# Windowed attention and a gated feed-forward on one core: values placed behind the next group's scores, sink values in two row halves, group 4 one unit sooner

## The chip, the core and the metric

The kernel runs on one core of a Trainium2 chip. The core has five engines with an instruction queue each: TensorE (PE) multiplies matrices, VectorE (DVE) and ScalarE (ACT) work on elements, GpSimd (POOL) and SyncE (SP) here mainly issue DMAs. Matmuls write to PSUM, which has eight banks of 128 partitions x 512 fp32 numbers. DMAs of all issuers run on 16 DMA engines; a DMA can also transpose a bf16 tile on its way, by the crossbar (xbar). The metric is the device time of one execution in microseconds (us); less is better. All times below are us unless marked ns.

## The reference

Inputs: q, k, v of 4 batches x 8 heads x 768 tokens x 64, and the weights of a gated feed-forward, 512 to 1536 and back. `n_sink` is 4, `window` is 128.

```python
keep = is_sink | in_window          # the first 4 keys, or the last 128 up to the query
scores = np.where(keep, scale * q @ k.T, -1e9)
a = softmax(scores)
x = (a @ v) as (4*768, 8*64)        # heads side by side
g = x @ w_gate
out = (g * sigmoid(g) * (x @ w_val)) @ w_out
```

## The kernel before

Attention goes in 12 groups of 256 query tokens; group g is third g%3 (called c) of batch g//3. The feed-forward goes in eight blocks `tb` of 256, 256, 256, 512, 512, 512, 512 and 256 tokens (`SIZES`): block 3 takes groups 3 and 4, block 4 takes 5 and 6, and so on. All orders are written by hand (`manual_schedule`): each engine runs its instructions in the order in which Python emits them.

A group's steps:

- Transposes of q and k: on TensorE (`step_T`) for groups 0 to 3, by a crossbar DMA issued by SyncE (`cross_T`, L301, tiles `kqT`) from group 4 on.
- `step_S(g, p2)`, scores of four heads (L331). Two heads run at once, each on 64 rows of the array. They take four PSUM banks `s`; ScalarE's exps (L338) empty these into `e`; VectorE's mask multiplications (L343) follow.
- `step_K(g)`, scores of the four sink keys of all heads (L358), with an exp into `es` (L362). Groups with c = 0 have none, since their sinks are in the window's tiles or in the mask.
- `step_PV(g, j, hh)`, values for half j of the group's tokens (128) and half hh of its heads (4), in one bank `o` (L384): where c > 0 a 128-row matmul of `es` with the sink values `vsb` (128x260), then eight matmuls of `e` with `va` (128x65; four where there is no earlier key tile). VectorE takes the reciprocal of the row sums (L389) and writes the scaled rows to `xn` (L396). `xn` has three buffers, one for each (g, j).
- The transpose of `xn` into the feed-forward's input `xT`: on TensorE (`step_X`, L420, bank `px`, and a copy) for groups below `NXPE` = 5 other than 3; by a crossbar DMA from SyncE (L402) for 3 and from 5 on.

A *gate unit* `gate(tb, f)` of a 512-token block is pg (four matmuls, L448), tanh `th` on ScalarE (L455), then pv (four matmuls, L448), and on VectorE `u` (L462, from `th` and pg) and `ht` (L463, from `u` and pv). A *down unit* `down(tb, ts)` is 12 matmuls over `ht` (L501), a scaled copy on ScalarE and a store. A block of 512 has units 0 to 11 (gates) and 12 to 15 (downs).

`weave` runs the units and puts attention steps into them: into a gate unit between pg and pv, into a down unit among its matmuls. `slots` says which steps go into which unit. A step's VectorE work is put on the list `later`, and is emitted (`flush`) after the unit's `u` and `ht`. So VectorE's order in a unit with scores and values is u, ht, masks, rcp, xn. In block 3 a values step of one (j, hh) stands in each of the units 6 to 9, in order (0,0), (1,0), (0,1), (1,1); scores of the group after stand in 8 and 10. PSUM tiles of all kinds share eight buffers (`bank`); a new tile takes one whose last reader has been emitted, longest ago first, and its first matmul waits for that reader.

The first group has its own code ahead of the blocks: transposes, scores, values, with `warm(n)`, n matmuls of zeros 512 wide whose result nobody reads, at places where TensorE waits. The list `us` then mixes blocks 0 to 2 (gates of 256 tokens, two chunks each) by hand; its units 15 to 20 are block 2's gates, 21 and 22 block 1's downs, 23 and 24 block 2's. There groups 1 to 4 have their steps: scores of group 4 in units 20 and 21, its values in 22 and 23, its transposes in 24.

Of the kernel before, what the change touches and what calls it, by code (L numbers as in the profile page):

```python
# [8 lines left out]
FP32 = mybir.dt.float32  # L9
# [6 lines left out]
def kernel(  # L16
# [12 lines left out]
    nc = tc.nc  # L29
    P = 128  # L30
    B, H, S, D = q.shape
# [9 lines left out]
    GC = S // 256  # L41
# [2 lines left out]
    assert sum(SIZES) == NTOK and NG == 12 and S == 768  # L44
    OFF = [sum(SIZES[:i]) for i in range(len(SIZES))]
    NPE = 4
    NXPE = 5
    VS = 72
    FCH = [2, 2, 2, 2, 4]
    assert sum(FCH) == DFC  # L50
# [29 lines left out]
    def bank(shape, dtype, name):  # L80
        return psum.tile(shape, dtype, tag="b", name=name)
# [70 lines left out]
    vsbs, kss = [], []  # L152
# [77 lines left out]
    kTs, qTs, es_t, e_t, xns, xTs = {}, {}, {}, {}, {}, {}  # L230
    later = []

    def A(fn, *a):
        return lambda: fn(*a)
# [6 lines left out]
    def warm(n):  # L241

        ps = bank([P, 512], FP32, "wm")
        for _ in range(n):
            nc.tensor.matmul(ps, wm[:, 0:P], wm, start=True, stop=True)
# [36 lines left out]
    def keys(b, t, r, p):  # L282

        g, j = b * GC + t // 2, t % 2
        if g < NPE:
            return kTs[g][r, p, j * P:(j + 1) * P]
        return cross[g][r, j, 0, p]

    def queries(g, r, p, j, n):

        if g < NPE:
            return qTs[g][r, p, j * P:(j + n) * P]
        return cross[g][r, j:j + n, 1, p]
# [3 lines left out]
    def cross_T(g):  # L297

        t = crossp.tile([P, 2, 2, NP2, P], BF16, tag="kqT", name="kqT")
        for j in range(2):  # L300
            nc.sync.dma_start(  # L301
                t[:, j].rearrange("q i a m -> q (i a) m"),
                nat[g][:, j].rearrange("p i x -> p (i x)"), transpose=True)
        cross[g] = t
# [10 lines left out]
    def step_S(g, p2, mid=None):  # L315

        b, c = divmod(g, GC)
        if p2 == 0:
            e_t[g] = epool.tile([P, H, 512], BF16, tag="e", name="e")

        parts = [(2 * c, 0, 2, P), (2 * c + 1, 1, 1, 3 * P)]
        if c > 0:
            parts.insert(0, (2 * c - 1, 0, 1, 0))
        lo = 0 if c > 0 else P
        pss = [bank([P, 512], FP32, "s") for _ in range(4)]
        for pp in range(2):
            p = 2 * p2 + pp
            for t, j, n, col in parts:
                for h in range(2):
                    r = slice(h * D, (h + 1) * D)  # L330
                    nc.tensor.matmul(  # L331
                        pss[2 * pp + h][:, col:col + n * P], keys(b, t, r, p),
                        queries(g, r, p, j, n), start=True, stop=True)
        m = (mask if c > 0 else mask0).rearrange("q (o a) x -> q o (a x)", o=1)
        for pp in range(2):
            h0 = 4 * p2 + 2 * pp
            for h in range(2):
                nc.scalar.activation(  # L338
                    e_t[g][:, h0 + h, lo:512], pss[2 * pp + h][:, lo:512],
                    AF.Exp, scale=scale)  # L340

            def dve(e=e_t[g][:, h0:h0 + 2, lo:512]):
                nc.vector.tensor_tensor(  # L343
                    e, e, m[:, :, lo:512].broadcast_to([P, 2, 512 - lo]), op=ALU.mult)
            later.append(dve)
            if pp == 0 and mid:
                mid()
# [17 lines left out]

    def step_PV(g, j, hh, act=False):
        b, c = divmod(g, GC)
        t = 2 * c + j
        if hh == 0:
            xns[g, j] = xnp.tile([P, DM], BF16, tag="xn", name="xn")  # L370
        po = bank([P, 4, D + 1], FP32, "o")
        mms = []
        if c > 0:
            mms.append((po, es_t[g][:, j * P:(j + 1) * P],
                        vsbs[b][:, 4 * hh:4 * hh + 4]))
        for hq in range(4):
            h = 4 * hh + hq
            if t > 0:
                vp = vas[g][:, 0, h, 0:D + 1] if j else vas[g - 1][:, 1, h, 0:D + 1]
                mms.append((po[:, hq], e_t[g][:, h, 256 * j:256 * j + P], vp))  # L380
            mms.append((po[:, hq], e_t[g][:, h, 256 * j + P:256 * (j + 1)],
                        vas[g][:, j, h, 0:D + 1]))
        for i, (o, l, r) in enumerate(mms):
            nc.tensor.matmul(o, l, r, start=(i == 0), stop=(i == len(mms) - 1),  # L384
                             skip_group_check=True)

        def dve():
            rcp = smallp.tile([P, 4, 1], FP32, tag="rcp", name="rcp")
            nc.vector.reciprocal(rcp, po[:, :, D:D + 1])  # L389
            if act:  # L390
                for h in range(4):
                    nc.scalar.activation(  # L392
                        xns[g, j][:, (4 * hh + h) * D:(4 * hh + h + 1) * D],
                        po[:, h, 0:D], AF.Copy, scale=rcp[:, h])
                return
            nc.vector.tensor_tensor(  # L396
                xns[g, j][:, 256 * hh:256 * (hh + 1)].rearrange(
                    "p (h d) -> p h d", h=4),
                po[:, :, 0:D], rcp.broadcast_to([P, 4, D]), op=ALU.mult)
        later.append(dve)  # L400
        if hh == 1 and (g >= NXPE or g == 3):
            later.append(lambda: nc.sync.dma_start(  # L402
                x_tile(g, j), xns[g, j], transpose=True))

# [3 lines left out]
    def x_tile(g, j):  # L408

        t0 = g * 256 + j * P  # L410
        tb = max(i for i in range(len(SIZES)) if OFF[i] <= t0)
        if t0 == OFF[tb]:
            xTs[tb] = xtp.tile([P, 4, DMC, P], BF16, tag="xT", name="xT")
        return xTs[tb][:, (t0 - OFF[tb]) // P]
# [99 lines left out]
    def gates(tb):  # L514
        return [(gate, tb, f) for f in range(0, DFC, 512 // SIZES[tb])]

    def downs(tb):
        return [(down, tb, t) for t in range(SIZES[tb] // P)]
# [6 lines left out]
    def sinks(b):  # L525
        return [lambda: later.append(A(step_ks, b))]
# [7 lines left out]
    def Ss(g):  # L534
        return [A(step_S, g, p2) for p2 in range(2)]

    def PVs(g):

        return [A(step_PV, g, j, hh) for hh in range(2) for j in range(2)]

    def Xs(g):
        return [A(step_X, g, j) for j in range(2)]

    def K(g):
        return A(step_K, g)
# [5 lines left out]
    def weave(us, slots):  # L551
        assert all(i < len(us) for i in slots)
        for i, (fn, tb, x) in enumerate(us):
            fn(tb, x, slots.get(i, []))
# [7 lines left out]
    def slots(*pairs):  # L562
        sl = {}
        for at, steps in pairs:
            for i, step in zip(at if isinstance(at, tuple) else (at,) * len(steps),
                               steps):
                sl.setdefault(i, []).append(step)
        return sl

    def C(g):  # L570

        def last():
            cross_T(g)
            next_load(g)
        return [last]
# [4 lines left out]
    def first_T(ph):  # L580
        transpose(0, ph, lambda i, p: first[p] if i else nat[0][:, 2 * p:2 * p + 2],
                  (ident, id32))

    build_masks()
    first_T(0)
    step_S(0, 0, A(first_T, 1))
    warm(1)
    step_S(0, 1)
    warm(2)
    last_mask = later.pop()  # L590
    flush()

    step_PV(0, 0, 0, True)
    step_PV(0, 1, 0, True)
    later.insert(1, last_mask)


# [3 lines left out]
    for i in range(3, 5):  # L601
        load_gate(i)
    step_PV(0, 0, 1)
    step_PV(0, 1, 1)
    step_T(1, 0, q_act=True)
    flush()
# [18 lines left out]
    def first_PVs():  # L625
# [8 lines left out]
    us = [g0[0], (held_gate, 0, 2), (alone, 0, 0), g0[2], *g1[0:3], g0[3], *g1[3:6], *g0[4:6],  # L634
          *downs(0), *g2, *downs(1), *downs(2)]
    weave(us, slots(
        (0, [flush, A(step_S, 1, 1), K(1), A(next_load, 1)]), (2, [first_PVs]),
        (3, [A(step_X, 1, 0), A(step_X, 1, 1, True), flush]),
        (9, T(2)), ((10, 11), Ss(2)), (10, [K(2)]),
        (12, PVs(2)[:2] + [flush]), (13, PVs(2)[2:] + [flush]), (13, C(4)),  # L640
        (14, [A(step_X, 2, 0), A(step_X, 2, 1, True), flush]),
        (15, T(3)), ((16, 17), Ss(3)), (17, sinks(1)), ((18, 18, 19, 19), PVs(3)), (19, [flush]),
        (18, C(5)), ((20, 21), Ss(4)), (21, [K(4)]),
        ((22, 22, 23, 23), PVs(4)), (24, Xs(4))))

    def pair(ga, gb, sh=0):
        s = sh
        return [((s, s + 2), Ss(ga)), ((s + 4, s + 5, s + 6, s + 7), PVs(ga)),
                ((s + 6, s + 8), Ss(gb)),
                ((11, 11, 12, 12) if s else (10, 11, 12, 13), PVs(gb))]  # L650

    weave(gates(3) + downs(3), slots(
        (2, [K(5)]), *pair(5, 6, 2), (2, C(6)), (7, C(7)), (13, C(8))))
    weave(gates(4) + downs(4), slots(
        (0, sinks(2)), *pair(7, 8), (3, [K(7)]), (3, C(9)), (7, C(10)), (10, C(11))))
    weave(gates(5) + downs(5), slots(
        (0, sinks(3)), *pair(9, 10), (6, [K(10)])))
    weave(gates(6) + gates(7) + downs(6) + downs(7), slots(
        ((0, 2), Ss(11)), ((4, 5, 6, 7), PVs(11))))


# [33 lines left out]
```

The softmax here doesn't subtract the row's maximum and nothing guards it: scores larger than these inputs give would overflow.

## Time and profile before

The time is 242.3 us (median of three runs, 241.95 to 242.7); the profiled execution has a span of 240.4.

| engine | busy | share of the span | instructions |
|---|---|---|---|
| TensorE matmul | 232.7 | 97% | 2071 |
| TensorE weight load (beside the matmuls) | 135.3 | 56% | 2071 |
| VectorE | 158.8 | 66% | 334 |
| ScalarE | 112.6 | 47% | 227 |
| GpSimd | 70.7 | 29% | 92 |

The costliest groups on TensorE are pg and pv (74.2 and 74.4 busy) and pd (63.4); the o matmuls have 18.2 for values and 8.8 for sinks, the px transposes 3.5. The granted TensorE clock is 0.71 from 12 to 13 us, 0.50 from 13 to 15, 0.58 from 15 to 16 and full otherwise. Busy times of matmuls overlap, since the next starts before the one ahead has drained: start-to-start times tell what a matmul costs. In lines of the timeline the columns are start, time to the last end, engine, line, operation with out<-in, and, in brackets, the engine's idle time before it and what ended that.

### The profile page before, as it was taken

How to read it: one execution, taken by the hardware profiler on the slowest of the kernel's cores; microseconds unless marked ns; L12 is line 12 of the kernel's file. 1: busy time of each engine (PE TensorE's matmuls, PEld its weight loads, DVE VectorE, ACT ScalarE, POOL GpSimd, SP SyncE). 2: the span in 40 equal slices, each digit the busy share in tenths (PEclk: the TensorE clock that was granted, in tenths of full speed). 3: DMA queues.
4: the chain of work that ended last, by engine and by line, in shares of the span. 5: the costliest groups of instructions: out<-in, count | busy, mean ns of one | idle time of the engine just before them, and what ended most of it. 6: DMA issues, size and time to landing. Idle time of an engine off the chain costs nothing.

```text
span 240.4 us, 5190 instructions
## 1 busy us (share of the span) xinstructions
PE 232.7 (97%) x2071; PEld 135.3 (56%) x2071; DVE 158.8 (66%) x334; ACT 112.6 (47%) x227; POOL 70.7 (29%) x92
## 2 busy tenths in 40 slices
PE   7799999999999999999999999999999999999994
PEld 3477887768745445454445454445454445488443
DVE  4569778939973589880698971498971599877000
ACT  2778447358451483621656611556611662332111
POOL 8985387686256745650000000000000000000000
PEclk9979999999999999999999999999999999999999
DMA  7999999999999999999920654200304200200132
GB/s 136 147 180 197 206 187 206 171 154 145 194 119 200 195 160 155 155 148 191 236 48 0 125 97 133 87 0 1 46 0 131 90 0 3 44 0 3 59 117 87
DMA packets 98793, 27.37 MB, mean 114 GB/s; under 512 B 84817, under 2 KB 95825, under 8 KB 98769
## 3 DMA queue, kind: packets, MB, share of 16 engines
q0 software_dynamic: 68832, 13.90, 71.5%
q1 hardware_dynamic: 29504, 12.75, 26.9%
q10 hardware_dynamic: 432, 0.39, 0.5%
q8 instruction: 16, 0.26, 0.5%
q14 instruction: 9, 0.07, 0.1%
HBM read 28.34 MB, written 6.29 MB: 144 GB/s over the span
## 4 chain that ended last, share of the span: by engine, by line
PE 87%; DVE 5%; ACT 3%; DMA 2%; issue 1%; DVEq 0%; ACTq 0%; POOLq 0%
PE pv L448 25%; PE pd L501 25%; PE pg L448 23%; PE o L384 5%; PE s L331 4%; PE pt L267 3%; ACT e L338 2%; DVE e L343 2%; DMA kq<-in_k_dram 2%; DVE ht L463 1%; DVE xn L396 1%; PE px L420 1%; DMA out_dram<-ot 1%; DVE u L462 1%; ACT xn L392 1%
## 5 line engine op out<-in xcount | busy, mean ns | idle before, releaser
L448 PE MATMUL pv<-xT,wv 128*128 128x256 bf16 (+1 forms) x384 | 74.4, 326 | 0.2 <-DVE xn L396 0.2
L448 PE MATMUL pg<-xT,wg 128*128 128x256 bf16 (+1 forms) x384 | 74.2, 326 | 0.0
L455 ACT ACTIVATE th<-pg 128x512 f32<-128x512 f32 x72 | 43.9, 609 | 59.7 <-PE pg L448 59.3
L462 DVE SCALAR_TENSOR_TENSOR u<-th,pg 128x512 bf16<-128x512 f32 x72 | 49.2, 683 | 30.5 <-ACT th L455 29.7
L501 PE MATMUL pd<-wo,ht 128*128 128x512 bf16 x276 | 63.4, 379 | 0.0
L463 DVE TENSOR_TENSOR ht<-u,pv 128x512 bf16<-128x512 bf16 x72 | 49.5, 687 | 10.2 <-PE pv L448 3.3
L448 PEld LDWEIGHTS <-wg 128*128 128x128 bf16 x384 | 37.4, 98 | 25.4 <-issue 0.2
L338 ACT ACTIVATE e<-s 128x512 bf16<-128x512 f32 (+1 forms) x96 | 46.3, 583 | 1.2 <-PE s L331 1.1
L448 PEld LDWEIGHTS <-wv 128*128 128x128 bf16 x384 | 34.1, 98 | 20.6 <-issue 2.7
L501 PEld LDWEIGHTS <-ht 128*128 128x128 bf16 x276 | 25.8, 98 | 28.0 <-issue 0.2
L505 ACT ACTIVATE ot<-pd 128x512 f32<-128x512 f32 x23 | 13.7, 597 | 53.0 <-PE pd L501 52.9
L343 DVE TENSOR_TENSOR e<-e,mask 128x1024 bf16<-128x1024 bf16 (+1 forms) x48 | 28.9, 641 | 1.2 <-ACT e L338 1.0
L123 POOL DMA_DIRECT2D va<-in_v_dram x24 | 21.2, 885 | 12.6 <-DMA kq<-in_q_dram 5.7
L384 PEld LDWEIGHTS <-e 128*128 128x128 bf16 x352 | 16.6, 99 | 6.7 <-DVE vcf L598 0.7
L396 DVE TENSOR_TENSOR xn<-o,rcp 128x256 bf16<-128x256 f32 x44 | 18.7, 424 | 2.5 <-DMA xT<-xn 1.0
L384 PE MATMUL o<-va,e 128*128 128x65 bf16 x352 | 18.2, 195 | 0.9 <-DVE vcf L598 0.5
L107 POOL DMA_DIRECT2D kq<-in_k_dram x16 | 14.1, 883 | 8.6 <-DMA kqT<-kq 4.5
L107 POOL DMA_DIRECT2D kq<-in_q_dram x16 | 14.1, 883 | 6.1 <-DMA va<-in_v_dram 2.9
L389 DVE RECIPROCAL rcp<-o 128x4 f32<-128x4 f32 x48 | 8.4, 176 | 6.8 <-PE o L384 6.8
L486 DVE TENSOR_SCALAR ot<-pd 128x256 f32<-128x256 f32 x1 | 0.4, 425 | 14.4 <-DMA out_dram<-ot 14.4
L331 PE MATMUL s<-kqT 64*128 64x128 bf16 (+1 forms) x168 | 9.4, 238 | 0.0
L272 DVE CAST qT<-pt 128x512 bf16<-128x512 f32 x7 | 4.7, 689 | 6.9 <-PE pt L267 6.9
(61 smaller groups left out, 107.5 us busy)
## 6 DMA issues: line engine op xcount, KB each, us to landing
out_dram<-ot SPq DMA_DIRECT2D x23, 256.0 KB
va<-in_v_dram POOLq DMA_DIRECT2D x24, 128.0 KB, 10.3
kq<-in_k_dram POOLq DMA_DIRECT2D x18, 128.0 KB, 9.3
kq<-in_q_dram POOLq DMA_DIRECT2D x16, 128.0 KB, 9.4
wo<-in_moe_w_out_dram POOLq DMA_DIRECT2D x4, 384.0 KB, 12.7
wg<-in_moe_w_gate_dram POOLq DMA_DIRECT2D x4, 256.0 KB, 8.7
wv<-in_moe_w_val_dram POOLq DMA_DIRECT2D x4, 256.0 KB, 9.1
kq<-in_k_dram POOLq DMA_DIRECT2D x3, 256.0 KB, 9.6
```

Of the source, the lines that this page charges most:

```text
L107: nc.gpsimd.dma_start(x[:, j, i].rearrange("p (h d) -> p h d", d=D), src[b, :, t0:t0 + P].rearrange("h m d -> m h d"))
L123: nc.gpsimd.dma_start(va[:, j, :, 0:D], v[b, :, t0:t0 + P].rearrange("h m d -> m h d"))
L331: nc.tensor.matmul(pss[2 * pp + h][:, col:col + n * P], keys(b, t, r, p), queries(g, r, p, j, n), start=True, stop=True)
L338: nc.scalar.activation(e_t[g][:, h0 + h, lo:512], pss[2 * pp + h][:, lo:512], AF.Exp, scale=scale)
L343: nc.vector.tensor_tensor(e, e, m[:, :, lo:512].broadcast_to([P, 2, 512 - lo]), op=ALU.mult)
L384: nc.tensor.matmul(o, l, r, start=(i == 0), stop=(i == len(mms) - 1), skip_group_check=True)
L396: nc.vector.tensor_tensor(xns[g, j][:, 256 * hh:256 * (hh + 1)].rearrange("p (h d) -> p h d", h=4), po[:, :, 0:D], rcp.broadcast_to([P, 4, ...
L448: nc.tensor.matmul(ps[:, i * n:(i + 1) * n], ws[fi][:, c, fo * P:(fo + 1) * P], x[:, 0:n // P, c], start=(c == 0), stop=(c == DMC - 1))
L455: nc.scalar.activation(th, pg, AF.Tanh, scale=0.5)
L462: nc.vector.scalar_tensor_tensor(u, th, 1.0, pg, op0=ALU.add, op1=ALU.mult)
L463: nc.vector.tensor_tensor(hts[tb][:, f:f + two].rearrange("p a n -> p (a n)"), u, pv, op=ALU.mult)
L501: nc.tensor.matmul(po, hts[tb][:, f, ts * P:(ts + 1) * P], wos[f // n][:, f % n], start=(f == 0), stop=(f == DFC - 1))
```

## The change

Five edits, all in the order or form of attention work:

1. A new `step_PV2(g, j)` takes both head halves of a token half. Where c > 0 it first issues the two sink matmuls with 64 rows each (heads 0 to 3 lie on rows 0 to 63 of `es` and `vsb`, heads 4 to 7 on rows 64 to 127), so that they can run side by side as the scores do, then the values of both halves.
2. From block 3 on, `step_PV2` replaces the four `step_PV`, and where it can it stands behind the scores of the following group in the same unit, so that the array, still split by rows, takes the sinks as well. The last scores and values move from block 6 into block 5.
3. Group 4's scores, sink scores and values come one unit sooner, and its output goes by crossbar DMA (`NXPE` = 3) and no more by `step_X`.
4. Fillers: `warm(3)` after the first transposes, `warm(3)` for `warm(1)`, `warm(2)` and `warm(3)` among group 0's values.
5. In unit 0 of `us`, K(1) stands ahead of scores (1,1).

```diff
-    NXPE = 5
+    NXPE = 3
...
+    def step_PV2(g, j):
+        b, c = divmod(g, GC)
+        pos = [value_bank(g, j, hh) for hh in range(2)]
+        if c > 0:
+            for hh in range(2):
+                r = slice(64 * hh, 64 * (hh + 1))
+                nc.tensor.matmul(
+                    pos[hh], es_t[g][r, j * P:(j + 1) * P],
+                    vsbs[b][r, 4 * hh:4 * hh + 4],
+                    start=True, stop=False, skip_group_check=True)
+        for hh in range(2):
+            values(g, j, hh, pos[hh])
...
-        if hh == 1 and (g >= NXPE or g == 3):
+        if hh == 1 and g >= NXPE:
...
     first_T(0)
+    warm(3)
     step_S(0, 0, A(first_T, 1))
-    warm(1)
+    warm(3)
     step_S(0, 1)
     warm(2)
...
     step_PV(0, 0, 0, True)
     step_PV(0, 1, 0, True)
+    warm(2)
...
     step_PV(0, 0, 1)
+    warm(3)
     step_PV(0, 1, 1)
...
-        (0, [flush, A(step_S, 1, 1), K(1), A(next_load, 1)]), (2, [first_PVs]),
+        (0, [flush, K(1), A(step_S, 1, 1), A(next_load, 1)]), (2, [first_PVs]),
...
-        (18, C(5)), ((20, 21), Ss(4)), (21, [K(4)]),
-        ((22, 22, 23, 23), PVs(4)), (24, Xs(4))))
-
-    def pair(ga, gb, sh=0):
-        s = sh
-        return [((s, s + 2), Ss(ga)), ((s + 4, s + 5, s + 6, s + 7), PVs(ga)),
-                ((s + 6, s + 8), Ss(gb)),
-                ((11, 11, 12, 12) if s else (10, 11, 12, 13), PVs(gb))]
+        (18, C(5)), ((19, 20), Ss(4)), (20, [K(4)]),
+        ((21, 21, 22, 22), PVs(4))))
+
+    def PV2s(g):
+        return [A(step_PV2, g, j) for j in range(2)]
 
     weave(gates(3) + downs(3), slots(
-        (2, [K(5)]), *pair(5, 6, 2), (2, C(6)), (7, C(7)), (13, C(8))))
+        (2, [K(5)]), ((2, 4), Ss(5)), (2, C(6)), (7, C(7)),
+        ((8, 10), Ss(6)), ((8, 10), PV2s(5)), ((11, 12), PV2s(6)), (13, C(8))))
     weave(gates(4) + downs(4), slots(
-        (0, sinks(2)), *pair(7, 8), (3, [K(7)]), (3, C(9)), (7, C(10)), (10, C(11))))
+        (0, sinks(2)), ((0, 2), Ss(7)), (3, [K(7)]), (3, C(9)),
+        ((6, 8), Ss(8)), ((6, 8), PV2s(7)), (7, C(10)), (10, C(11)),
+        ((10, 12), Ss(9)), ((10, 12), PV2s(8))))
     weave(gates(5) + downs(5), slots(
-        (0, sinks(3)), *pair(9, 10), (6, [K(10)])))
-    weave(gates(6) + gates(7) + downs(6) + downs(7), slots(
-        ((0, 2), Ss(11)), ((4, 5, 6, 7), PVs(11))))
+        (0, sinks(3)), ((1, 3), PV2s(9)), ((2, 4), Ss(10)), (5, [K(10)]),
+        ((7, 9), Ss(11)), ((7, 9), PV2s(10)), ((11, 12), PV2s(11))))
+    weave(gates(6) + gates(7) + downs(6) + downs(7), {})
```

More of the change, by code (lines that the diff above doesn't have):

```diff
@@ L367, in step_PV, with value_bank, values @@
         b, c = divmod(g, GC)
-        t = 2 * c + j
+        po = value_bank(g, j, hh)
+        if c > 0:
+            nc.tensor.matmul(
+                po, es_t[g][:, j * P:(j + 1) * P], vsbs[b][:, 4 * hh:4 * hh + 4],
+                start=True, stop=False, skip_group_check=True)
+        values(g, j, hh, po, act)
+    def step_PV2(g, j):
+        b, c = divmod(g, GC)
+        pos = [value_bank(g, j, hh) for hh in range(2)]
+        if c > 0:
+            for hh in range(2):
+                r = slice(64 * hh, 64 * (hh + 1))
+                nc.tensor.matmul(
+                    pos[hh], es_t[g][r, j * P:(j + 1) * P],
+                    vsbs[b][r, 4 * hh:4 * hh + 4],
+                    start=True, stop=False, skip_group_check=True)
+        for hh in range(2):
+            values(g, j, hh, pos[hh])
+    def value_bank(g, j, hh):
         if hh == 0:
             xns[g, j] = xnp.tile([P, DM], BF16, tag="xn", name="xn")
-        po = bank([P, 4, D + 1], FP32, "o")
+        return bank([P, 4, D + 1], FP32, "o")
+    def values(g, j, hh, po, act=False):
+        b, c = divmod(g, GC)
+        t = 2 * c + j
         mms = []
-        if c > 0:
-            mms.append((po, es_t[g][:, j * P:(j + 1) * P],
-                        vsbs[b][:, 4 * hh:4 * hh + 4]))
         for hq in range(4):
@@ L383, in step_PV @@
         for i, (o, l, r) in enumerate(mms):
-            nc.tensor.matmul(o, l, r, start=(i == 0), stop=(i == len(mms) - 1),
-                             skip_group_check=True)
+            nc.tensor.matmul(o, l, r, start=(c == 0 and i == 0),
+                             stop=(i == len(mms) - 1), skip_group_check=True)
         def dve():
```

## The prediction

> **What bounds the kernel now.** I read the page first, then the waits of TensorE, then TensorE, VectorE and ScalarE in order of time in the three blocks of 512 tokens (78.7 to 211 us).
>
> ```profile
> PE 232.7 (97%) x2071; PEld 135.3 (56%) x2071; DVE 158.8 (66%) x334; ACT 112.6 (47%) x227; POOL 70.7 (29%) x92
> ...
> PE 87%; DVE 5%; ACT 3%; DMA 2%; issue 1%; DVEq 0%; ACTq 0%; POOLq 0%
> ```
>
> TensorE is busy for 97% of the span and is 87% of the chain that ended last. Its own waits (all named ones together 4.2 us) lie before 25 us, but for 0.2 us at 64.6. So after 25 us the end moves by what is taken from TensorE's work, or put into it as waits. TensorE in block 4:
>
> ```profile
> 118.61 1.03 PE L448 MATMUL pg<-xT,wg 128*128 128x512 bf16 x4
> 119.57 0.62 PE L331 MATMUL s<-kqT 64*128 64x128 bf16 x12
> 120.12 1.04 PE L448 MATMUL pv<-xT,wv 128*128 128x512 bf16 x4
> 120.99 1.03 PE L448 MATMUL pg<-xT,wg 128*128 128x512 bf16 x4
> ...
> 123.16 1.03 PE L448 MATMUL pg<-xT,wg 128*128 128x512 bf16 x4
> 124.02 0.27 PE L384 MATMUL o<-vsb,es 128*128 128x260 bf16 x1
> 124.13 0.41 PE L384 MATMUL o<-va,e 128*128 128x65 bf16 x8
> 124.38 1.02 PE L448 MATMUL pv<-xT,wv 128*128 128x512 bf16 x4
> ```
>
> Read starts only. Half a gate (4 matmuls) is 0.865 (120.12 to 120.99). So pg of 118.61 is through at 119.475; scores come 0.095 later (119.57), run 0.43 (1024 columns at the dense rate) and give back after another 0.12 (120.12): 0.65 in all. A values step is 0.36: sinks 0.11 and eight times 0.031. Beside it, VectorE and ScalarE:
>
> ```profile
> 97.54 0.69 DVE L463 TENSOR_TENSOR ht<-u,pv 128x512 bf16<-128x512 bf16 x1 [0.45 <-PE pv L448]
> 98.14 0.17 DVE L389 RECIPROCAL rcp<-o 128x4 f32<-128x4 f32 x1
> 98.35 0.42 DVE L396 TENSOR_TENSOR xn<-o,rcp 128x256 bf16<-128x256 f32 x1
> 98.69 1.02 DVE L343 TENSOR_TENSOR e<-e,mask 128x768 bf16<-128x768 bf16 x2
> 99.63 0.68 DVE L462 SCALAR_TENSOR_TENSOR u<-th,pg 128x512 bf16<-128x512 f32 x1
> 100.41 0.69 DVE L463 TENSOR_TENSOR ht<-u,pv 128x512 bf16<-128x512 bf16 x1
> ```
>
> ```profile
> 95.78 0.60 ACT L455 ACTIVATE th<-pg 128x512 f32<-128x512 f32 x1 [1.48 <-PE pg L448]
> 96.40 1.64 ACT L338 ACTIVATE e<-s 128x384 bf16<-128x384 f32 x4
> ```
>
> VectorE keeps program order. u to ht is 0.79, ht to the next 0.60 (1.39 a gate), a mask 0.47 (0.60 at 1024 wide), rcp and xn 0.55, xn written 0.62 after rcp starts. ht starts 0.20 after its pv ends (97.34), and masks and xn stand behind it. th starts 0.20 after pg ends (95.58), the exps behind it.
>
> ```profile
> 72.88 0.42 DVE L396 TENSOR_TENSOR xn<-o,rcp 128x256 bf16<-128x256 f32 x1 [1.04 <-DMA xT<-xn]
> ```
>
> ```profile
> 64.02 2.51 SPq L402 DMA_TRANSPOSE xT<-xn  x2
> ```
>
> These two say how slow the crossbar is here: xn has 3 buffers, so this xn (group 4, second half of tokens) waits for group 3's first transpose, issued at 64.02 and landed at 72.8: 8.8 us.
>
> **What the Trainium skill says.** "TensorEngine Tiling (Array Packing)", Key Properties: changing the tiling mode drains TensorE. The trace agrees: 0.10 into and about 0.12 out of 64-row scores. "TensorE: Matmul & The Clock Gate", Part 1: the clock halves when the array was little used over a window of about 3.4 us. The trace agrees: clock 0.50 to 0.71 between 12 and 16 us, after the gaps of 9 to 12. "DMA: Bandwidth & Descriptors", Issuing engines are not separate DMA queues: transfers of all issuers interleave on the same 16 engines. The trace agrees: 8.8 us above, with GpSimd's loads running, against 2.5 us for the one issued at 136.63 after they ended.
>
> **The change part by part.**
>
> *Row-shared sinks.* Two sink matmuls of 0.11 become two of 64 rows at once: 0.11 saved per step. Seven of the ten with sinks stand behind scores and share their drains: -0.77. Three ((8,1), (11,0), (11,1)) stand alone and pay 0.20 for entering and leaving: +0.09 each. Together **-0.5**.
>
> *Values behind scores.* The matmuls are the same, but one unit now takes pg, four score banks, two value banks and pv: all eight PSUM banks. VectorE gets 1.39+1.20+1.10 = 3.69 us in it, TensorE has 2.97. The built program shows whose release each matmul waits for:
>
> - Block 4 units 8 and 10, block 5 unit 9: the second sink matmul takes the bank of this unit's first score tile, so it waits for the first exp. That ends 0.20+0.60+0.03+0.60 = 1.43 after pg ends (1.33 for 384 columns); TensorE is there after 0.095+0.43 = 0.53 (0.42). With 0.05 for the release that is 0.92 to 0.96 each: **+2.8**. Behind it are 16 values matmuls, then pv.
> - Block 3 unit 10: the second sink matmul takes unit 9's pg bank, freed by u. With pg of unit 8 at 0: pv8 ends 2.87, ht8 3.07, masks 3.67, rcp/xn 4.61, u9 5.71, written 6.39. TensorE is there at 5.88: **+0.55**.
> - Block 3 unit 11: values of group 6, heads 4 to 7, need the masks of unit 10. From pv10's end: ht 0.20, masks at 0.80 and 1.27, written 1.78. TensorE, after pg and 4 matmuls, is there at 0.99: **+0.8**. Before, heads 0 to 3 of both token halves came in this slot and heads 4 to 7 a unit later.
> - Block 5 unit 4: pv waits for ht of unit 3, which xn of unit 1 and masks of unit 2 delay: **+0.2**.
>
> *Group 4 a unit sooner.* Two transposes by TensorE go (76.48 to 76.71 and 77.57 to 77.80): -0.46, the wait at 64.6 with the score half before it (-0.37), one mode change around K (-0.1). New: scores of group 4 stand behind group 3's last values, and the pv behind them takes the bank of o of step (3,1,0). VectorE writes that xn at 63.41 in the trace (62.99+0.42), and nothing ahead of it there moves; pv would come at 62.37: **+1.1**. es of group 4 now stands behind four exps on ScalarE: th to 66.0, exps to 67.9, es to 68.4; the values want it at 67.8: **+0.65**. So block 3 would ask for its input at 78.66+0.8 = 79.4.
>
> *Its output by crossbar.* xn (4,1) still can't start before 72.88, as group 3's transposes are where they were. Behind it on VectorE: 0.34, then 0.55 and 0.62 for the other half: xn written at 74.4. SP issues (4,0) at 73.9 and (4,1) at 75.2 (1.2 each). From issue to landing: 8.8 by the line above; output stores issued at 73 to 79.5 landed after 5.7 to 6.6 by the trace's semaphores; 2.5 when nothing else runs. So (4,1) lands between 77.7 (no wait) and 83.9. I take 7.3, between the stores and the transpose: 82.5. The first pg of block 3 waits for all four tiles, and all of TensorE is behind it. Block 3 starts at 82.5 in place of 78.66: **+3.8**, which takes in the +0.8.
>
> *Fillers and K first.* 13 fillers for 3. Those at 6.5, 8.9, 10.2 and 11.3 lie in TensorE's gaps (qT to 7.26, qT to 9.68, the masks to 11.67); the three between the last two values steps (0.65) are on the path, beside q's load until 13.0. If they keep the clock, transposes and px of 13.2 to 16.0 take half: about 1.1 sooner, but then wg1 (landed 18.6) and wv1 (20.0) bound: pv at 20.05 as now. What stays is es ahead of the exps (0.36) and 0.2 at xn: **-0.5**. If the clock still drops: +0.6. Either is mostly swallowed by the wait for (4,1), since DMAs set that.
>
> **Sum.** 3.8 at block 3, 2.8+0.55+0.8+0.2 = 4.35 in the blocks, -0.5 for the sinks: +7.65. 242.3+7.65 = 249.9, say **249.8 us**.
>
> **The rivals.**
> - *The transpose lands in time* (245 to 248). For it: 2.5 us on an idle queue. Against: the DMA engines are at 0.9 or more until 120 us in the page. Then 0.8-0.5+4.35-0.5 = +4.2: 246.5. Chance 0.22.
> - *The waits are hidden*: banks come free earlier than I count, and only TensorE's work counts. -0.46-0.47-0.5-0.5 = -1.9: 240.4, faster. For it: none of these waits is in the trace of before. Against: there heads and token halves are spread one step to a unit. Chance 0.07.
> - *The clock drops too*: TensorE stands for some 3 us at block 3, as long as the gaps that halved it at 12 us; 3.4 us at half speed is +1.7: 251.5. Chance 0.13.
> - Nothing measurable, by gains and waits of about 2 us each: 0.02.
>
> **How the numbers follow.** The forecast itself has 0.56. The range goes from 245.0, with the landing in time and a part of the bank waits hidden, to 252.0, with the clock lost. Faster 0.07, same 0.02, slower 0.91.
>
> **What would show it.** In the profile after: TensorE waits for DMA xT<-xn (2 to 5 us) at the first pg of block 3; for ACT e or es, and for DVE u, xn and e, at the o matmuls of blocks 3 to 5, with 0.9 us three times; at 62 to 64 us pv waits for xn. TensorE's busy time is lower, its share too. I am wrong if the o matmuls follow the scores without a gap, or if group 4's transposes land within 4 us.

## The result, and the profile after

The changed kernel took 249.7 us (median of 4 runs, 248.45 to 250.93) beside 242.5 us for the kernel before (4 runs): ratio 1.030, 95% interval 1.0241 to 1.0356. Run again later, beside 11 runs of before, it took 248.6 us (5 runs, 247.41 to 248.84): ratio 1.025, interval 1.0224 to 1.0269. So it is 6 to 7 us slower. The profiled run below is the slowest of the first four, the one of 250.9 us, with a span of 249.2 us; before had 240.4.

The page of the changed kernel, first TensorE's busy time, then the clock by slice (10 is written as 9), then the chain by engine:

```profile
PE 236.0 (95%) x2060; PEld 133.8 (54%) x2073; DVE 158.0 (63%) x332; ACT 113.0 (45%) x227; POOL 70.7 (28%) x92
...
PEclk9999999999999799999999999999999999999999
...
PE 65%; DMA 25%; DVE 3%; ACT 3%; issue 1%; POOL 1%; SPq 0%; ACTq 0%; DVEq 0%
```

TensorE's busy time is 3.3 us more; ten fillers more (2.2 us at 0.216 each) and the halved clock of one slice (1.3 us, below) are in it, so it says little of the work. That slice, at 81 to 87 us, is the 7 in the second line. The chain now goes through DMA for a quarter of the span, where it was 2%: something that comes by DMA is waited for. TensorE's waits name it (us in total, times, longest):

```profile
PE pg L470 <- DMA xT<-xn: 3.4, 1, 3.4
...
PE o L382 <- ACT e L338: 1.1, 3, 0.4
...
PE o L406 <- DVE e L343: 0.5, 2, 0.3
...
PE o L382 <- DVE u L484: 0.3, 1, 0.3
```

The first is block 3's first gate, the others are values steps in blocks 3 to 5. In before, TensorE's only named wait after 25 us is one of 0.2 us at 64.6. In order of time, at the start of block 3:

```profile
82.61 1.86 PE L470 MATMUL pg<-xT,wg 128*128 128x512 bf16 x4 [3.38 <-DMA xT<-xn]
84.27 1.55 PE L470 MATMUL pv<-xT,wv 128*128 128x512 bf16 x4
85.66 1.03 PE L470 MATMUL pg<-xT,wg 128*128 128x512 bf16 x4
```

Read starts: the first two half gates take 1.66 and 1.39 us in place of 0.865 each. After the wait of 3.4 us TensorE ran at half speed, which cost another 1.3 us. The granted clock is 0.50 from 81.9 to 85.3 us, 3.4 us in all, of which the first 0.7 fell into the wait and cost nothing.

Then block 4, units 6 and 8, which hold the same instructions:

```profile
134.01 0.62 PE L331 MATMUL s<-kqT 64*128 64x128 bf16 x12
134.47 0.28 PE L382 MATMUL o<-vsb,es 64*128 64x260 bf16 x2
134.67 0.66 PE L406 MATMUL o<-va,e 128*128 128x65 bf16 x16
...
138.72 0.62 PE L331 MATMUL s<-kqT 64*128 64x128 bf16 x12
139.28 0.28 PE L382 MATMUL o<-vsb,es 64*128 64x260 bf16 x1
139.96 0.27 PE L382 MATMUL o<-vsb,es 64*128 64x260 bf16 x1 [0.40 <-ACT e L338]
140.16 0.66 PE L406 MATMUL o<-va,e 128*128 128x65 bf16 x16
```

In unit 6 both sink matmuls go together and the values follow 0.20 later. In unit 8 the second one stands alone at 139.96, released by an exp of its own unit's scores. It reads es and no result of these scores: by the order of the built program, it wants the PSUM bank of the first score tile. From pg to pv is 2.12 us in unit 6 (133.05 to 135.17) and 2.90 in unit 8 (137.76 to 140.66). So the wait costs 0.78; the idle time of 0.40 that the line gives is less, as it leaves out the drain of the matmuls before.

Where the 8.8 us of span went can be laid out by three starts: pg of unit 19 of the mixed list (the last one ahead of everything done to group 4), the first pg of block 3, the first pg of block 6. All are from the traces, in us (spans to two places: 240.44, 249.23 and 247.13):

| kernel | unit 19 to block 3 | block 3 to block 6 | block 6 to end |
|---|---|---|---|
| before | 18.06 | 108.77 | 53.01 |
| changed | 22.16 | 116.46 | 50.16 |
| changed, run again | 21.02 | 115.12 | 50.15 |

Ahead of unit 19 the changed kernel was 0.15 sooner. Then +4.10, +7.69 and -2.85. The last is group 11's scores and values, which stood in block 6 before; so the new layout costs 115.12-108.77-2.86 = 3.5 us, and the clock 116.46-115.12 = 1.34. The run without clock loss gives 2.96+3.5 = 6.5, and the measured spans differ by 6.7. Block 3 to block 6 repeats closely where nothing in it was edited: 115.12 to 115.14 us in six profiles that kept the clock. That makes it a sharper measure than the medians. The stretch ahead of it moves with the landing, and the last one by some 0.15 us.

### The profile page after: what moved, and what is told of

Read it like the earlier page. It is cut to its first block, busy times and chain, and to the rows that moved or that the text cites. A ratio compares the mean times of both kernels' runs of the same rounds, so it can differ in the third digit from the quotient of the medians.

```text
span 249.2 us, 5186 instructions
## 1 busy us (share of the span) xinstructions
PE 236.0 (95%) x2060; PEld 133.8 (54%) x2073; DVE 158.0 (63%) x332; ACT 113.0 (45%) x227; POOL 70.7 (28%) x92
## 4 chain that ended last, share of the span: by engine, by line
PE 65%; DMA 25%; DVE 3%; ACT 3%; issue 1%; POOL 1%; SPq 0%; ACTq 0%; DVEq 0%
PE pv L470 19%; PE pg L470 18%; PE pd L523 18%; DMA xT<-xn 6%; DMA wv<-in_moe_w_val_dram 5%; DMA wo<-in_moe_w_out_dram 5%; DMA kqT<-kq 4%; PE o L406 3%; DMA kq<-in_q_dram 3%; PE s L331 2%; PE wm L245 2%; ACT e L338 2%; PE pt L267 1%; DVE e L343 1%; DVE xn L418 1%
## 5 line engine op out<-in xcount | busy, mean ns | idle before, releaser
L470 PE MATMUL pg<-xT,wg 128*128 128x256 bf16 (+1 forms) x384 | 75.0, 328 | 3.4 <-DMA xT<-xn 3.4
L470 PE MATMUL pv<-xT,wv 128*128 128x256 bf16 (+1 forms) x384 | 74.8, 328 | 0.6 <-DMA wv<-in_moe_w_val_dram 0.4
L523 PE MATMUL pd<-wo,ht 128*128 128x512 bf16 x265 | 61.4, 379 | 0.5
L470 PEld LDWEIGHTS <-wv 128*128 128x128 bf16 x384 | 35.5, 98 | 24.2 <-issue 3.5
L123 POOL DMA_DIRECT2D va<-in_v_dram x24 | 21.2, 888 | 12.4 <-DMA kq<-in_q_dram 6.4
L406 PEld LDWEIGHTS <-e 128*128 128x128 bf16 x352 | 14.0, 97 | 8.0 <-issue 3.4
L406 PE MATMUL o<-va,e 128*128 128x65 bf16 x352 | 16.4, 194 | 1.1 <-DVE vcf L622 0.5
L331 PEld LDWEIGHTS <-kqT 64*128 64x128 bf16 x168 | 5.5, 94 | 6.7 <-issue 6.4
```

The costliest lines, as they stand in the source:

```text
L123: nc.gpsimd.dma_start(va[:, j, :, 0:D], v[b, :, t0:t0 + P].rearrange("h m d -> m h d"))
L331: nc.tensor.matmul(pss[2 * pp + h][:, col:col + n * P], keys(b, t, r, p), queries(g, r, p, j, n), start=True, stop=True)
L406: nc.tensor.matmul(o, l, r, start=(c == 0 and i == 0), stop=(i == len(mms) - 1), skip_group_check=True)
L470: nc.tensor.matmul(ps[:, i * n:(i + 1) * n], ws[fi][:, c, fo * P:(fo + 1) * P], x[:, 0:n // P, c], start=(c == 0), stop=(c == DMC - 1))
L523: nc.tensor.matmul(po, hts[tb][:, f, ts * P:(ts + 1) * P], wos[f // n][:, f % n], start=(f == 0), stop=(f == DFC - 1))
```

## The experiments

### Group 4's output by TensorE

```diff
-    NXPE = 3
+    NXPE = 5
-        if hh == 1 and g >= NXPE:
+        if hh == 1 and (g >= NXPE or g == 3):
-        ((21, 21, 22, 22), PVs(4))))
+        ((21, 21, 22, 22), PVs(4)), (23, Xs(4))))
```

> The changed kernel, with group 4's output turned by TensorE as before (its two transposes in the unit after its last values), everything else left as changed, group 4 one unit sooner too. Theory (the crossbar's late landing holds block 3): the 3.4 us wait ahead of block 3's first gate goes, and with it the halved clock of the slice after (gates there took 1.66 and 1.39 us in place of 0.865: 1.3 us); two transposes come back (0.46). Block 3 starts at 79 to 80 us in place of 82.6, and the time falls by 4 to 5 us against the changed kernel: 245 to 246. Rival (block 3 waits for something that lands late in any case, a weight or group 3's transposes): it stays within 1 us of the changed kernel, 249 to 250.

246.8 us, ratio to before 1.018 (1.0164 to 1.0197). Block 3's first gate had no wait, the clock was 1.00, unit 19 to block 3 took 19.08 us and block 3 to block 6 115.13, as in the changed kernel run again. The late landing holds block 3, as the theory has it. The gain is 2.9 us against the first measurement of the changed kernel and 1.8 against the second, less than the 4 to 5 expected: I had worked from a run with the longest wait and the lost clock.

### Blocks 3 to 5 as before

```diff
-    def PV2s(g): ...
+    def pair(ga, gb, sh=0): ...
-        (2, [K(5)]), ((2, 4), Ss(5)), (2, C(6)), (7, C(7)),
-        ((8, 10), Ss(6)), ((8, 10), PV2s(5)), ((11, 12), PV2s(6)), (13, C(8))))
+        (2, [K(5)]), *pair(5, 6, 2), (2, C(6)), (7, C(7)), (13, C(8))))
...
```

> The changed kernel with blocks 3 to 5 laid out as before: values one step to a unit, away from scores, and sinks over 128 rows; start, group 4 and the crossbar as changed. Theory (bank and mask waits cost 3.5 to 4.4 us, row-shared sinks give 0.5): 3.5 to 4 us faster than the changed kernel, 245.7 to 246.2, still about 3.5 slower than before. Rival (the waits in the o matmuls only move work that the late start of block 3 would delay anyway): within 1 us of the changed kernel.

244.5 us, 1.010 (1.0064 to 1.0137). Block 3 to block 6 is 108.76 us and the rest 52.89, those of before. So the layout's cost goes wholly. It is 5.2 us faster than the first measurement of the changed kernel and 4.1 than the second; what is over 3.5 lies ahead of block 3, where the landing differs from run to run (unit 19 to block 3: 20.77 here).

### The new layout alone

Start and group 4 of the kernel before, blocks 3 to 5 of the changed one (the reverse of the last diff, with the start's fillers left out).

> The kernel before with only the new layout of blocks 3 to 5: values of a token half behind the scores of the next group, row-shared sinks. Start and group 4 as before. Theory (bank waits of 0.8 to 0.9 us three times, 0.55 and 0.85 in block 3, less 0.5 for the sinks): 3.3 to 4 us slower than before, 245.8 to 246.5. Rival (only TensorE's work counts): 0.5 to 1 us faster than before.

245.9 us, 1.0135 (1.0114 to 1.0155): 3.3 us. Unit 19 to block 3 is 18.06, block 3 to 6 115.14. Layout and start-up add up: 3.3 here, and 2.0 for everything else in the experiment above, make 5.3 of the 6.2 of the changed kernel measured again. The 0.9 that are left are no more than the landing differs between runs (20.55 to 22.22 us from unit 19 to block 3, below).

### Fillers and K first alone

```diff
     first_T(0)
+    warm(3)
     step_S(0, 0, A(first_T, 1))
-    warm(1)
+    warm(3)
...
-        (0, [flush, A(step_S, 1, 1), K(1), A(next_load, 1)]), (2, [first_PVs]),
+        (0, [flush, K(1), A(step_S, 1, 1), A(next_load, 1)]), (2, [first_PVs]),
```

> The kernel before with only the fillers at the start and K(1) ahead of the score half. Theory (wv's landing at 20 us sets the start, the clock gained there ends in a wait): 0.1 to 0.4 us faster than before, 242.1 to 242.4. Rival (the clock of 12 to 16 us set the start): about 1.1 us faster, 241.4. Rival (fillers lie on the path): 0.6 us slower.

242.1 us beside 242.6, ratio 0.999 (0.9976 to 1.0003): not to be told from no change. Both rivals, 1.1 us faster and 0.6 slower, lie outside the interval. The clock between 12 and 16 us is 1.00 (0.57 in before), in the profile of this kernel (busy time of five engines with counts, then the clock):

```profile
12.00:16.00 4.00, 3.23 (x90) 2.42 (x92) 2.39 (x10) 2.54 (x10) 2.52 (x4) 1.00 1.72 169
```

and what was gained ends in a wait for a weight, in TensorE's order of time:

```profile
19.73 1.05 PE L448 MATMUL pg<-xT,wg 128*128 128x256 bf16 x8 [0.56 <-DMA wg<-in_moe_w_gate_dram]
```

### Five buffers for xn

```diff
-    xnp = pool("xnp", 3)
+    xnp = pool("xnp", 5)
```

> The changed kernel with 5 buffers for xn in place of 3, so that group 4's xn no longer waits for group 3's transposes to land. Theory (two landings in a row set block 3: group 3's free the buffers, then group 4's go out and take about 6.8 us): (4,1) is issued at 74.0 in place of 75.8 and lands at 80.5 to 81; the wait at block 3 falls from 3.4 to about 1.6 us and the clock holds: 1.8 to 3.1 us faster than the changed kernel, 246.6 to 247.9. Rival (the place in the queue behind the loads sets the landing, not the issue): landing stays at 82 to 83, within 0.5 us of the changed kernel.

248.0 us, 1.0236 (1.0205 to 1.0266). (4,1), the transpose for group 4's second token half, was issued at 73.73 and landed at 80.61, the wait was 1.7 us, the clock held: as expected for the profile. But this does not show that the buffers did it. In the experiment with fillers at block 3, with 3 buffers, group 3's first transpose happened to land at 71.4, (4,1) went out at 73.75 and landed at 80.80, the same. The buffers can help only where group 3 lands after about 71.4, as in the changed kernel's two profiles (73.4 and 72.4, issue at 75.8 and 74.8). Against its second measurement the gain is 0.6 us, within its spread.

### Without the late loads, twice

```diff
         x = natp.tile([P, 2, 2, H * D], BF16, tag="kq", name="kq")
+        if g >= 8:                      # second kernel: g >= 6
+            nc.gpsimd.memset(x, 0.0)
+            nat[g] = x
+            return
...
+        if g >= 8:                      # in load_v as well
+            nc.gpsimd.memset(va[:, :, :, 0:D], 0.0)
+            return
```

> The changed kernel without the loads of k, q and v for groups 8 to 11 (their tiles are filled with zeros by GpSimd, so four of the twelve groups are computed on zeros), otherwise the same work. Theory (the transposes are slow because GpSimd's loads stand in the same DMA engines): group 4's transposes land 2.5 to 4 us after issue, block 3 starts at 78.5 to 79.5 without a wait, the clock holds: 4 to 5 us faster than the changed kernel, 245 to 246. Rival (the crossbar or SP's own queue of transposes is slow at that point by itself): landing still 6 to 7 us after issue, within 1 us of the changed kernel.

249.1 us, 1.0266 (1.0229 to 1.0303), (4,1) lands 6.81 us after issue. By these numbers the rival was right; but the kernel did not make its condition. Loads of groups 6 and 7 were still landing until 82.6 us. A transpose issued after that, of a later group's q and k, landed sooner: issued at 83.56, landed at 87.74. So the second kernel also left out groups 6 and 7:

> The changed kernel without the loads of k, q and v for groups 6 to 11 (tiles filled with zeros by GpSimd; half of the groups computed on zeros), otherwise the same work. Without the loads of groups 8 to 11 alone, those of groups 6 and 7 were still landing until 82.6 us and group 4's transposes took 6.8 us as before; transposes issued after that took 4.2. Theory (the transposes wait in the DMA engines among GpSimd's loads): with the loads through by 70 us, group 4's transposes land 2.5 to 4 us after issue, that is before 78.8 us; no wait at block 3, the clock holds, block 3 starts at 78.5 to 79.2: 244.5 to 245.5. Rival (the transposes are slow by themselves at that point): landing 6 to 7 us after issue, 248 to 250.

245.7 us, 1.0141 (1.0122 to 1.0159), 0.2 over the range of the theory and far below the rival's. (4,1) was issued at 73.81 and landed at 76.27: 2.46 us. SP's issues of the two transposes in the changed kernel, and then in this one:

```profile
74.53 2.50 SPq L424 DMA_TRANSPOSE xT<-xn  x2
```

```profile
72.53 2.50 SPq L431 DMA_TRANSPOSE xT<-xn  x2
```

The issue itself takes the same 2.50 us. What differs is the landing, 6.67 and 2.46 us after the second issue. TensorE in the kernel without loads:

```profile
72.88 6.21 PE L530 MATMUL pd<-wo,ht 128*128 128x512 bf16 x28
78.92 1.03 PE L477 MATMUL pg<-xT,wg 128*128 128x512 bf16 x4
79.78 1.03 PE L477 MATMUL pv<-xT,wv 128*128 128x512 bf16 x4
```

The gate follows the downs with no wait and at full speed. So it is GpSimd's loads in flight that make the transposes land late, here by 4.2 us. The Trainium skill says in "DMA: Bandwidth & Descriptors", Issuing engines are not separate DMA queues, that the DMAs of all issuers run on the same 16 engines and interleave; these two kernels agree with that. They do not tell a wait in the engines from a wait for the memory behind them. With loads in flight, unit 19 to block 3 takes 20.55 to 22.22 us in eight profiles, here 18.62: the late landing costs 1.9 to 3.6 us, besides the clock.

### Fillers inside the wait at block 3

```diff
+    warm(10)
     weave(gates(3) + downs(3), slots(
```

> The changed kernel with 10 filler matmuls (0.216 us each, 2.2 us) between the last down of block 2 and block 3's first gate, inside the wait for the transposes. Theory (the 3.4 us stall also cost clock): block 3 starts when it did, its first gates run at full speed (0.865 each in place of 1.66 and 1.39): 1.3 us faster than the changed kernel, 248.4. Rival (the slow first gates are not a matter of an idle TensorE): no gain, within 0.4 us.

248.3 us, 1.0246 (1.0213 to 1.028). The mean clock was 1.00 in all five runs. But in the profile (4,1) landed at 80.8, so this run would have had a short wait anyway; against the changed kernel's second measurement the gain is 0.3 us, within its spread. So it decides nothing. What says more is the next one.

### The changed kernel again

> The changed kernel as it is, run beside the others, to see how its time spreads. Theory (group 4's last transpose lands at 80.6 or 82.5 us, and only the longer wait halves the clock): times fall in two groups, about 248 with the clock at 1.00 and 249 to 251 with a mean clock of 0.993. Rival: one group around 249.7, with no tie to the clock.

All five kept the clock: 247.4 to 248.8 us. With the first four, those with a mean clock of 1.00 took 247.4 to 248.8 (6 runs) and those with 0.993 took 249.4 to 250.9 (3 runs). So the slower runs are those that lost clock. But the groups are only 0.5 us apart and each spreads over 1.4 or more, and a run with five xn buffers took 249.6 us at a clock of 1.00: the clock is not all that varies, the landing does too. The profile of a run that kept the clock:

```profile
81.86 1.02 PE L470 MATMUL pg<-xT,wg 128*128 128x512 bf16 x4 [2.24 <-DMA xT<-xn]
82.72 1.03 PE L470 MATMUL pv<-xT,wv 128*128 128x512 bf16 x4
```

The gates take 0.86 here. The landing was at 81.7, between the two that I had named.

### Values one unit later, away from the scores

```diff
-        ((8, 10), Ss(6)), ((8, 10), PV2s(5)), ((11, 12), PV2s(6)), (13, C(8))))
+        ((8, 10), Ss(6)), ((9, 11), PV2s(5)), ((12, 12), PV2s(6)), (13, C(8))))
-        ((6, 8), Ss(8)), ((6, 8), PV2s(7)), (7, C(10)), (10, C(11)),
-        ((10, 12), Ss(9)), ((10, 12), PV2s(8))))
+        ((6, 8), Ss(8)), ((7, 9), PV2s(7)), (7, C(10)), (10, C(11)),
+        ((10, 12), Ss(9)), ((11, 12), PV2s(8))))
-        ((7, 9), Ss(11)), ((7, 9), PV2s(10)), ((11, 12), PV2s(11))))
+        ((7, 9), Ss(11)), ((8, 10), PV2s(10)), ((11, 12), PV2s(11))))
```

> The changed kernel with the two-half values steps of blocks 3 to 5 one unit later, in units that hold no scores (group 6's both in the first down unit), sinks over 64 rows as changed. Theory (the waits come from eight banks and the vector work of one unit together): the five waits of blocks 3 to 5 (0.55, 0.85 and three of 0.78) go, 3.7 us; seven steps no longer share the scores' mode change, about 0.22 each, 1.5 us back. Net 2.2 us faster than the changed kernel, about 247.5. Rival (the waits come from two halves of a step in a row, wherever it stands): the waits stay and the mode changes are added, 1 to 1.5 us slower than the changed kernel.

248.5 us, 1.0233 (1.0186 to 1.0279), from 246.4 with the clock kept to 249.5 with it lost. All waits of o matmuls in blocks 3 to 5 are gone. A values unit of block 4:

```profile
136.12 0.28 PE L382 MATMUL o<-vsb,es 64*128 64x260 bf16 x2
136.33 0.66 PE L406 MATMUL o<-va,e 128*128 128x65 bf16 x16
136.83 1.02 PE L470 MATMUL pv<-xT,wv 128*128 128x512 bf16 x4
```

Both sinks together again. This profile lost more clock than any: its first three half gates of block 3 took 1.66, 1.71 and 1.70 us in place of 0.865 and the fourth 1.12, together 2.7. Block 3 to block 6 is 115.61, less 2.7 is 112.9: 2.2 us under the changed kernel, as expected. The medians show it less well, since four of the six runs lost clock, three of them twice as much. The two that kept it took 246.4 and 246.6, some 2 us under the six such runs of the changed kernel.

### Sinks over 128 rows, in the same place

```diff
     def PV2s(g):
-        return [A(step_PV2, g, j) for j in range(2)]
+        return [lambda j=j: [step_PV(g, j, hh) for hh in range(2)] for j in range(2)]
```

> The changed kernel with each two-half values step as two ordinary ones in the same place: sink matmul over 128 rows and eight values for heads 0 to 3, then the same for heads 4 to 7. So the second value bank is asked for 0.36 us later. Row-shared theory: 0.11 more in each of seven steps behind scores, 0.09 less in each of three that stand alone: +0.5. Bank theory: the four waits for a bank (0.78 three times, 0.55) shrink by what now stands ahead of them, 0.25 net of the 0.11, in each: units with a wait last 2.65 in place of 2.90 us, those without 2.23 in place of 2.12. Sum 0.7 us faster than the changed kernel between the starts of blocks 4 and 6. Rival (the second half waits for data, not for a bank): the waits keep their length, 0.5 us slower.

247.2 us, 1.0217 (1.0189 to 1.0245). Block 3 to block 6 is 113.80, 1.3 us less than the changed kernel; 1.1 of it after the start of block 4, where 0.7 was expected. Unit 8 of block 4:

```profile
138.01 0.28 PE L370 MATMUL o<-vsb,es 128*128 128x260 bf16 x1
138.13 0.41 PE L406 MATMUL o<-va,e 128*128 128x65 bf16 x8
138.69 0.27 PE L370 MATMUL o<-vsb,es 128*128 128x260 bf16 x1
```

Eight values now run while the exp frees the bank. From pg to pv 2.55 us (136.49 to 139.04), in place of 2.90. In units without a wait it is 2.23 in place of 2.12 (131.67 to 133.90). So sharing rows saves 0.11 where nothing waits and loses 0.35 where a bank is short, since it asks for both banks at once. The wait is for the bank and not for data: the first sink matmul reads the same rows of es here and runs at 138.01, so es is there, and yet the second starts at 138.69, 2.20 us after pg as in the changed kernel (137.76 to 139.96). In both, this is 0.04 to 0.05 after the end of the first exp, which frees the bank of the first score tile. The forecast of 0.7 had the units with a wait at 2.65.

No version here beats the kernel before by more than its measurement can tell.

## Why the prediction was right

The forecast was 249.8 us by a late crossbar, waits for banks, and small gains. Step by step:

- **Row-shared sinks, -0.5: right for the matmuls, not for the edit.** 0.11 behind scores (2.12 against 2.23). Alone they lose 0.10: unit 11 of block 5 takes 1.67 from pg to pv with them and 1.57 with 128 rows. But they also ask for both banks at once, which lengthens the waits. Taken together, 64 rows made blocks 3 to 5 longer by 1.3 us than 128 rows in the same place (115.12 against 113.80). The forecast booked the waits under the place of the values alone; both have a part in them.
- **Second sink behind the first exp, 0.92 to 0.96 three times: right in kind, too large.** Measured 0.78 or 0.79 each. The term that was off is th to the first exp, taken as 0.63. ScalarE of the changed kernel in unit 8:

```profile
138.82 0.60 ACT L477 ACTIVATE th<-pg 128x512 f32<-128x512 f32 x1 [1.13 <-PE pg L470]
139.32 2.06 ACT L338 ACTIVATE e<-s 128x512 bf16<-128x512 f32 x4
```

  They start 0.50 apart: an instruction's 0.60 overlaps the next by 0.1.
- **The other waits: right.** Block 3 unit 10, +0.55: 0.55 (2.55 from pg to pv, 2.00 in unit 8). Unit 11, +0.8: 0.85. Block 5 unit 4, +0.2: 0.2. All waits together are 3.95 us; less 0.47 for seven shared steps at -0.11 and three at +0.10, that is the 3.5 us of the layout, so nothing of size is left over. The changed kernel, block 3:

```profile
105.72 0.27 PE L382 MATMUL o<-vsb,es 64*128 64x260 bf16 x1 [0.28 <-DVE u L484]
...
108.70 0.24 PE L406 MATMUL o<-va,e 128*128 128x65 bf16 x2 [0.27 <-DVE e L343]
109.16 0.23 PE L406 MATMUL o<-va,e 128*128 128x65 bf16 x2 [0.23 <-DVE e L343]
```

- **Group 4 a unit sooner, +0.8 with TensorE's transposes gone: somewhat too large.** Without loads in the way it is 18.62-18.06 = +0.56. The transposes are 0.46 as forecast (19.08-18.62). What stood last ahead of unit 19's pv differed by run: xn in some traces, as forecast, and in others, the profiled run among them, the landing of kqT ahead of the scores (0.74 us at 62.76), which the forecast did not have.
- **Output by crossbar, block 3 at 82.5 us: right.** 82.6 and 81.9 in the two profiles. The forecast's +3.8 lies high in what was found: +4.1 and +3.0, and in the other kernels with this crossbar +2.5 to +2.8, once +4.2. From issue to landing I took 7.3; it was 6.7 to 7.05 in eight profiles. The issue, forecast for 75.2, came between 73.7 and 75.8, as group 3's transposes landed. The cause that I gave, GpSimd's loads, was an argument then; the kernel without them shows it.
- **Fillers, -0.5 and swallowed: right** in that the clock held and the gain ended in a wait for weights. The size is not shown: alone they gave 0.5 us with an interval that takes in no change, and in the changed kernel unit 19 began at 60.45 and 60.84, in before at 60.60.
- **The clock.** I made its loss at block 3 a rival with 0.13. It is part of what happened: 3 of the 9 runs of the changed kernel lost it, at some 1.3 us, and three of the first four. That the forecast of 249.8 met 249.7 so closely is in part luck, since errors offset: the three bank waits were 0.45 too dear and the landing 0.8 in the second profile, while no clock loss was counted. With the clock kept the kernel takes about 248.5.
- **Two signs failed.** TensorE's busy time was to be lower and is 3.3 us higher, since ten fillers and the half clock are in it. And in the profiled run no pv waits for xn at 62 to 64 us; it does in other traces.

## What to carry to other kernels

Before two jobs are put in one stretch, count the PSUM banks that it holds and ask when the last one comes free: a matmul that reads ready data can still wait for a bank, and asking for banks one after the other hides part of that. A transfer that TensorE's next block needs is to be timed with the loads that share the DMA engines, not alone. To read an edit's worth from noisy medians, compare stretches between fixed instructions.

## What the runs showed of the hardware that was not expected

- The clock is lost in whole portions. The runs that lost it show mean clocks of 0.993 and 0.986: 0.007 of 249 us at half speed is 3.5 us, 0.014 of 248 us is 6.9 us, twice as long. The Trainium skill gives a window of about 3.4 us that runs freely ("TensorE: Matmul & The Clock Gate", Part 1), and the portions agree.
- Whether a stall costs a portion depends on more than its length. A wait of 2.0 us at block 3 lost one in the kernel without groups 8 to 11, waits of 2.1 and 2.2 us in two others lost none, the two of 3.4 us lost one and two. Where the wait falls explains this. In each trace the records of the clock, from the first at full speed to the fall after the last matmuls, begin whole steps of 3.41 us apart: in the changed kernel at 6.83, 81.92 and 85.33 us, 22 steps and one. Lay these steps over the waits at block 3. Where TensorE was idle for 1.98 us or more within one step, the clock halved at its end (2.68 in the changed kernel, 2.18 with values one unit later, 1.98 without groups 8 to 11). Where a wait left 1.81 us or less in a step, a full clock held: 1.81 with blocks as before, 1.60 with five buffers, and 1.47 and 1.17 where the edge of a step cut the 2.2 and the 2.1 us in two. A clock that was already half came back after a step with 0.7 us idle and not after one with 1.26. This fits all seven profiles with a wait there. It is not the whole measure: at the start of before, from 9.0 to 12.4 us, where the matmuls are short, 1.38 us of idle time in a step was enough. How the chip counts is not shown.
- A crossbar transpose of one xn tile takes 2.5 us from issue to landing with quiet DMA engines. With loads in flight (4,1) took 6.7 to 7.05 us in eight profiles, and group 3's transposes, issued at about 64 us, up to 8.8.
- ScalarE starts exps 0.49 us apart that are listed with 0.60 us each.
